# Moving the weight tiles of a three-stage kernel by 128 bytes in SBUF

## The chip, the cores and the metric

One Trainium2 chip, one core. The metric is the device time of one execution in microseconds; the kernel before takes 1165.19 us in the median of three runs (1164.79 to 1169.47). Lower is better.

## What is computed

Two sequences of 4096 positions with 192 channels go through a causal convolution with 7 taps per head (the taps are a softmax over the given weights), and then through two feed-forward layers, one with SiLU and one with ELU, each with an inner width of 2048. Everything is float32.

```python
w = softmax(weight, axis=-1)                      # 8 heads x 7 taps
out = einsum('hk,bskhg->bshg', w, windows(x, 7))  # causal, 24 channels a head
x = out.reshape(8192, 192)
h = x @ w_in;  x = (h * sigmoid(h)) @ w_out       # layer 0
h = x @ w_in2; x = elu(h) @ w_out2                # layer 1
```

## The kernel before

**Tiling.** The 8192 positions are cut into NB = 16 blocks of TB = 512 (`b`). The inner width 2048 is cut into NQ = 8 parts of 256 (`q`). A unit is one (layer, b, q); there are 2 x 16 x 8 = 256 units, and they run layer by layer, block by block, part by part. The loop near the end of the file issues, for each step, the input products of one unit and the output products of the unit two steps earlier (LAG = 2).

**Products.** Each number is held as a high and a low part in the type float32r, so that a product is built from three products of parts. `in_products` (L297, the matmul at L309) makes 9 matmuls for each half of the rows, `out_products` (L339, the matmul at L352) 10; a step of the loop therefore has 2 x 19 = 38 matmuls. Each multiplies 64 rows: one stream uses partitions 0 to 63, the other partitions 64 to 127, and matmuls of the two streams are issued in turn (`products`), so that one of each is under way. Each has a stationary operand (`lhsT`) of 64 partitions x 128 float32 columns, loaded by an instruction of its own, LDWEIGHTS (engine PEld in the rows), and a moving operand (`rhs`) of 64 partitions x 512 float32 columns. The whole program has 256 x 38 + 20 = 9748 matmuls, 20 of them in `warm` (L511).

**Operands.** The stationary operands are slices of the weight tiles `wi` and `wo`, the moving ones slices of `x_hl` (layer input) for L309 and of `g_hi` and `g_lo` (activations, high and low part) for L352. ScalarE and VectorE make `g_hi` and `g_lo` from the PSUM tile `h`.

**Weights on their way.** `load_w` (L83) brings float64 words into a `raw` tile by DMA. `decode_steps` (L97) turns them into float32: ScalarE writes the magnitude into `mag` (L109), VectorE builds the value in `val` (L112, L115, L119). `split_w` (L129) writes the high part to `wi` or `wo` with ScalarE (L126, L140) and the low part with GpSimd or VectorE (L127, L142). For parts 3 to 6 of layer 1 the value is built in other tiles, `val_g` (from the pool `tmp`) and `val_x` (from `xin`).

**Places in SBUF.** Tiles of a partition lie one behind the other in the order of the pools (L58 to L68), each rounded up to 32 bytes: `const` (with `tap_m`, `tap_s`, `tap_r` last), `wts`, `raw`, `mag_p`, `dec`, `xin`, `xs`, `out_p`, `mid`, `gp`, `tmp`. The pool `wts` starts at 416 modulo 512. A `wi` or `wo` tile has 2 x 384 x 4 = 3072 bytes, six times 512, so all 18 of them, and every 128-column slice of them (512 bytes), start at 416 modulo 512. So do the `raw` tiles (6144 bytes each), `mag` and the `val` tiles (3072 bytes each) and the first `x_raw` tile. The two `x_raw` tiles of 4160 bytes move the place on by 128, so `xs` and everything behind it start at 32 modulo 512: `x_hl`, `g_hi`, `g_lo`, `val_g`, whose slices of 512 columns have 2048 bytes, four times 512. Every moving operand thus starts at 32 modulo 512, every stationary operand at 416.

Of the kernel before, what the change touches and what calls it, by code (L numbers as in the profile page):

```python
# [9 lines left out]
F32 = mybir.dt.float32  # L10
# [12 lines left out]
P = 128  # L23
# [6 lines left out]
W_IN = 3 * P  # L30
W_OUT = 2 * D
RAW = 3

PLACES = NQ + 1


@with_exitstack
def kernel(
# [19 lines left out]
    const = ctx.enter_context(tc.tile_pool(name="const", bufs=1))  # L58
    wts = ctx.enter_context(tc.tile_pool(name="wts", bufs=1))
    raw = ctx.enter_context(tc.tile_pool(name="raw", bufs=RAW))  # L60
    mag_p = ctx.enter_context(tc.tile_pool(name="mag_p", bufs=1))
# [19 lines left out]
    IN, OUT, BOTH = slice(0, W_IN), slice(W_IN, W_IN + W_OUT), slice(0, W_IN + W_OUT)  # L81
# [11 lines left out]
    def words(layer, q, cols):  # L93
        w = raw_t[layer, q].bitcast(I32).rearrange("p (n two) -> p n two", two=2)
        return w[:, cols, 0], w[:, cols, 1]

    def decode_steps(layer, q, cols, val=None, mag=None):  # L97


        if (layer, q) not in dec_t:  # L100
            if mag is None:
                mag = mag_p.tile([P, W_IN + W_OUT], F32, tag="mag", name="mag")
            if val is None:
                val = dec.tile([P, W_IN + W_OUT], I32, tag="val", name="val")
            dec_t[layer, q] = mag, val
        mag, val = (t[:, cols] for t in dec_t[layer, q])
        lower, upper = words(layer, q, cols)
        return [
            lambda: nc.scalar.activation(  # L109
                out=mag, in_=upper.bitcast(F32), func=ACTF.Abs, scale=2.0**-112  # L110
            ),
            lambda: nc.vector.tensor_scalar(  # L112
                out=val, in0=lower, scalar1=29, scalar2=None, op0=ALU.logical_shift_right
            ),
            lambda: nc.vector.scalar_tensor_tensor(  # L115
                out=val, in0=upper, scalar=-(2**31), in1=val,
                op0=ALU.bitwise_and, op1=ALU.bitwise_or,
            ),
            lambda: nc.vector.scalar_tensor_tensor(  # L119
                out=val, in0=mag.bitcast(I32), scalar=3, in1=val,  # L120
                op0=ALU.logical_shift_left, op1=ALU.bitwise_or,
            ),
        ]
# [5 lines left out]
    def split_w(layer, q, cols, eng):  # L129
        if (layer, q) not in wt:  # L130
            wt[layer, q] = [
                wts.tile([P, 2, n], F32R, tag=f"{t}{(layer * NQ + q) % PLACES}", name=t)
                for t, n in (("wi", W_IN), ("wo", W_OUT))
# [13 lines left out]
    tap_raw = const.tile([P, 2, TAPS], F32, name="tap_raw")  # L147
    tap_e = const.tile([P, 2, TAPS], F32, name="tap_e")
    tap_w = const.tile([P, 2, TAPS], F32, name="tap_w")
    tap_m = const.tile([P, 2], F32, name="tap_m")  # L150
    tap_s = const.tile([P, 2], F32, name="tap_s")
    tap_r = const.tile([P, 2], F32, name="tap_r")

# [264 lines left out]
    def next_w(layer, q, *others, val=None):  # L418
        run(decode_steps(layer, q, BOTH, val), *others)
        if q + RAW < NQ:  # L420
            load_w(layer, q + RAW)
# [7 lines left out]
    def first_step(q):  # L429
        steps_w[q] = decode_steps(0, q, BOTH)  # L430
        return steps_w[q][1]
# [36 lines left out]
    base = where[0, NB - 1, 0]  # L468
    spare = PLACES - NQ
    for q in range(NQ):  # L470
# [11 lines left out]
    with tc.manual_schedule():  # L482
# [7 lines left out]
        ab = conv_steps(0, 0, lambda: ps_h.tile([P, 2, TB], F32, tag="h", name="conv")[:, 0, :])  # L490
        c, c_1 = conv_pool_steps(0, 1), conv_pool_steps(1, 1)
        d_in, d_out = (decode_steps(0, 0, cols) for cols in (IN, OUT))
        run(ab, c)
        run(c_1[:4])
# [122 lines left out]
```

## Time and profile before

| | before |
|---|---|
| median of 3 runs | 1165.19 us (1164.79 to 1169.47) |
| profiled execution, span from first to last instruction | 1167.4 us |
| matmuls under way (PE) | 1143.8 us, 98% |
| weight loads under way (PEld) | 942.9 us, 81% |
| VectorE, ScalarE, GpSimd busy | 70%, 55%, 5% |
| mean granted clock of TensorE | 0.998 |
| share of the chain that ended last | TensorE 96% |

All rows below are of one profiled execution. PE is TensorE's matmuls and PEld its weight loads, which overlap them; L309 is line 309 of the kernel; `h<-x_hl,wi` names what is written and what is read; 64*128 are the active rows and columns and 64x512 the shape that is read. Two matmuls are always under way, one of each stream, so what counts is how far apart the starts of one stream are, not how long a matmul's own row is.

### The profile page before, as it was taken

The page shows a single profiled execution, that of the slowest core. Times are in us where ns is not written, and L with a number is a line of the kernel's source. Part 1 is how long each engine was busy: PE and PEld are TensorE (multiplying, and loading weights), DVE is VectorE, ACT ScalarE, POOL GpSimd, SP SyncE. Part 2 cuts the span into 40 slices and gives each one's busy share as a digit, 9 for nine tenths or more (in the row PEclk, how much of TensorE's full clock was granted, in tenths as well). Part 3 has the DMA queues.
Part 4 walks back from the last instruction along what each step waited for, and adds up shares of the span by engine and source line. Part 5 has one row for each costly group of instructions (what it writes and reads, how often), then busy time and mean ns, then how long its engine had stood idle before and what let it go on. Part 6 is the DMA issues. An engine that isn't in the chain of part 4 may idle for free.

```text
span 1167.4 us, 22505 instructions
## 1 busy us (share of the span) xinstructions
PE 1143.8 (98%) x9748; PEld 942.9 (81%) x9748; DVE 819.8 (70%) x957; ACT 645.2 (55%) x761; POOL 57.5 (5%) x67
## 2 busy tenths in 40 slices
PE   4899999999999999999999999999999999999998
PEld 3799999977777777777789777777777777777776
DVE  8965546556556555567767787877878777787876
ACT  7655455555545555456775455555455554555554
POOL 7500000000000000000320000000000000000000
PEclk9999999999999999999999999999999999999999
DMA  6310111110111110152300111101111101111100
GB/s 189 105 47 9 34 42 42 42 37 6 42 42 42 42 25 18 42 136 82 83 10 29 33 42 42 42 16 35 33 42 42 42 15 28 42 42 42 30 22 19
DMA packets 31188, 51.11 MB, mean 44 GB/s; under 512 B 3952, under 2 KB 13936, under 8 KB 31088
## 3 DMA queue, kind: packets, MB, share of 16 engines
q1 hardware_dynamic: 31088, 49.67, 16.5%
q8 instruction: 76, 1.25, 0.5%
q14 instruction: 24, 0.20, 0.1%
HBM read 18.98 MB, written 6.29 MB: 22 GB/s over the span
## 4 chain that ended last, share of the span: by engine, by line
PE 96%; DVE 2%; issue 0%; SPq 0%; DMA 0%; ACT 0%; POOL 0%; DVEq 0%
PE h L309 46%; PE ab L352 30%; PE c L352 20%; DVE val L112 0%; DVE val L115 0%; DVE g_lo L337 0%; DMA raw<-in_w_dram 0%; DVE x_hl L127 0%; SPq L187 0%; DVE val L119 0%; DVE conv L268 0%; SPq L87 0%; POOL wi L127 0%; ACT x_hl L126 0%; DVE x_hl L229 0%
## 5 line engine op out<-in xcount | busy, mean ns | idle before, releaser
L309 PE MATMUL h<-x_hl,wi 64*128 64x512 f32 x4608 | 747.1, 394 | 19.7 <-ACT wi L126 13.5
L309 PEld LDWEIGHTS h<-x_hl,wi 64*128 64x128 f32 x4608 | 566.5, 184 | 116.5 <-ACT wi L126 13.9
L352 PE MATMUL ab<-g_hi,wo 64*128 64x512 f32 x2048 | 445.2, 392 | 0.0
L352 PEld LDWEIGHTS ab<-g_hi,wo 64*128 64x128 f32 x2048 | 319.7, 184 | 41.3
L352 PE MATMUL c<-g_lo,wo 64*128 64x512 f32 x1024 | 305.7, 392 | 0.0
L352 PE MATMUL c<-g_hi,wo 64*128 64x512 f32 x1024 | 305.4, 392 | 0.0
L352 PE MATMUL ab<-g_lo,wo 64*128 64x512 f32 x1024 | 305.4, 392 | 0.0
L337 DVE TENSOR_TENSOR g_lo<-h,g_hi 128x1024 fp32r<-128x1024 f32 x128 | 156.6, 1223 | 175.4 <-ACT h L326 175.3
L325 ACT ACTIVATE g_hi<-h 128x1024 fp32r<-128x1024 f32 x128 | 131.3, 1026 | 241.5 <-PE h L309 241.5
L330 ACT ACTIVATE g<-h 128x1024 f32<-128x1024 f32 x128 | 131.7, 1029 | 238.8 <-PE h L309 237.0
L332 DVE SCALAR_TENSOR_TENSOR g<-g,h 128x1024 f32<-128x1024 f32 x128 | 156.0, 1219 | 91.2 <-ACT g L331 90.9
L352 PEld LDWEIGHTS c<-g_hi,wo 64*128 64x128 f32 x1024 | 182.4, 184 | 20.7
L352 PEld LDWEIGHTS c<-g_lo,wo 64*128 64x128 f32 x1024 | 182.4, 184 | 20.6
L352 PEld LDWEIGHTS ab<-g_lo,wo 64*128 64x128 f32 x1024 | 182.4, 184 | 20.5
L337 DVE TENSOR_TENSOR g_lo<-g,g_hi 128x1024 fp32r<-128x1024 f32 x128 | 156.9, 1226 | 4.5
L331 ACT ACTIVATE g<-g 128x1024 f32<-128x1024 f32 x128 | 135.9, 1061 | 3.5
L326 ACT ACTIVATE h<-h 128x1024 f32<-128x1024 f32 x128 | 130.8, 1022 | 0.0
L268 DVE SCALAR_TENSOR_TENSOR conv<-x_raw,tap_w,conv 128x512 f32<-128x512 f32 (+1 forms) x180 | 106.0, 628 | 0.5
L335 DVE CAST g_hi<-g 128x1024 fp32r<-128x1024 f32 x128 | 88.8, 694 | 4.5
L374 DVE TENSOR_TENSOR both<-c,both 128x512 f32<-128x512 f32 x32 | 22.1, 692 | 52.2 <-ACT both L373 52.2
L127 POOL TENSOR_TENSOR wi<-val,wi 128x384 fp32r<-128x384 f32 x11 | 11.6, 1055 | 532.0 <-ACT wi L126 532.0
L127 DVE TENSOR_TENSOR x_hl<-conv,x_hl 64x256 fp32r<-64x256 f32 (+1 forms) x47 | 23.9, 534 | 1.2 <-ACT x_hl L126 0.7
(61 smaller groups left out, 325.3 us busy)
## 6 DMA issues: line engine op xcount, KB each, us to landing
x_hl<-x_hl SPq DMA_DIRECT2D x76, 256.0 KB, 3.9
raw<-in_w_dram SPq DMA_DIRECT2D x16, 512.0 KB, 4.4
x_hl<-x_hl SPq DMA_DIRECT2D x34, 128.0 KB, 3.7
x_raw<-in_xT_dram SPq DMA_DIRECT2D x16, 259.0 KB, 3.8
raw<-in_w_dram SPq DMA_DIRECT2D x32, 128.0 KB, 3.2
out_dram<-o SPq DMA_DIRECT2D x16, 256.0 KB, 2.0
x_raw<-in_xT_dram SPq DMA_DIRECT2D x32, 65.5 KB, 3.0
out_dram<-other SPq DMA_DIRECT2D x16, 128.0 KB, 2.3
```

The lines of the kernel that those rows point to most:

```text
L127: eng.tensor_sub(out=lo, in0=src, in1=hi.bitcast(F32))
L268: nc.vector.scalar_tensor_tensor(out=y, in0=x, scalar=w, in1=y, op0=ALU.mult, op1=ALU.add)
L309: nc.tensor.matmul(out=h[:, r, :], lhsT=w[ROWS[r], w_lo, ts(of, P)], rhs=x[ROWS[r], 3 * x_lo + part, :], start=n == 0, stop=n == len(order ...
L325: lambda: nc.scalar.activation(out=hi, in_=h, func=ACTF.Silu),
L326: lambda: nc.scalar.activation(out=g, in_=h, func=ACTF.Silu),
L330: lambda: nc.scalar.activation(out=g, in_=h, func=ACTF.Relu, scale=-1.0),
L331: lambda: nc.scalar.activation(out=g, in_=g, func=ACTF.Exp, scale=-1.0),
L332: lambda: nc.vector.scalar_tensor_tensor(out=g, in0=g, scalar=-1.0, in1=h, op0=ALU.add, op1=ALU.max),
L335: lambda: nc.vector.tensor_copy(out=hi, in_=g),
L337: return steps + [lambda: nc.vector.tensor_sub(out=lo, in0=g, in1=hi.bitcast(F32))]
L352: nc.tensor.matmul(out=acc_t[layer, b, f"{name}{r}"], lhsT=wo[ROWS[r], i, cols], rhs=hi_lo[part][ROWS[r], i, :], start=q == 0 and n in (0, ...
L374: nc.vector.tensor_add(out=to[:, cols], in0=halves[1][:, cols], in1=to[:, cols])
```

## The change

The tile `tap_m` in the pool `const` grows by 128 bytes per partition; only its first two elements are used, as before. Everything behind it moves on by 128 bytes: `tap_s`, `tap_r`, the weight tiles, the `raw` tiles and the start of `mag`. The tile `mag` grows by 3 x 128 = 384 bytes, which are not used. The tiles behind `mag` thus move by 128 + 384 = 512 bytes and keep their place modulo 512. No instruction is added, removed or moved, and no shape changes.

```diff
@@ -32,6 +32,7 @@
 RAW = 3
 
 PLACES = NQ + 1
+LINE = 128
 
@@ -99,7 +100,8 @@
         if (layer, q) not in dec_t:
             if mag is None:
-                mag = mag_p.tile([P, W_IN + W_OUT], F32, tag="mag", name="mag")
+                mag = mag_p.tile([P, W_IN + W_OUT + 3 * LINE // 4], F32, tag="mag", name="mag")
+                mag = mag[:, BOTH]
@@ -147,7 +149,7 @@
-    tap_m = const.tile([P, 2], F32, name="tap_m")
+    tap_m = const.tile([P, 2 + LINE // 4], F32, name="tap_m")[:, 0:2]
```

## Rows read from the trace of the kernel before

**Rows 1.** The page's span, and busy time of each engine.
```profile
span 1167.4 us, 22505 instructions
PE 1143.8 (98%) x9748; PEld 942.9 (81%) x9748; DVE 819.8 (70%) x957; ACT 645.2 (55%) x761; POOL 57.5 (5%) x67
```
**Rows 2.** The page's chain that ended last, share by engine, then by line.
```profile
PE 96%; DVE 2%; issue 0%; SPq 0%; DMA 0%; ACT 0%; POOL 0%; DVEq 0%
...
PE h L309 46%; PE ab L352 30%; PE c L352 20%; DVE val L112 0%; DVE val L115 0%; DVE g_lo L337 0%; DMA raw<-in_w_dram 0%; DVE x_hl L127 0%; SPq L187 0%; DVE val L119 0%; DVE conv L268 0%; SPq L87 0%; POOL wi L127 0%; ACT x_hl L126 0%; DVE x_hl L229 0%
```
**Rows 3.** The chain in order of time: start us, length us, engine, line.
```profile
5.52 4.26 DMA raw<-in_w_dram
...
54.87 2.12 PE h L309 x12
...
63.76 2.10 PE h L309 x18
68.19 2.10 PE h L309 x18
...
613.49 1.63 PE h L309 x14
617.92 1.64 PE h L309 x14
```
**Rows 4.** Stretches: length, busy us (instructions) by engine, granted clock, DMA share, GB/s.
```profile
0.00:30.00 30.00, 14.31 (x82) 10.68 (x84) 25.75 (x35) 22.19 (x40) 21.94 (x28) 0.94 0.65 184
300.00:600.00 300.00, 300.00 (x2574) 238.17 (x2572) 180.10 (x238) 168.76 (x206) 18.58 (x21) 1.00 0.19 50
600.00:900.00 300.00, 300.00 (x2574) 244.90 (x2572) 241.31 (x250) 166.46 (x182) 2.15 (x3) 1.00 0.14 35
```
**Rows 5.** Timeline of the last matmuls: start us, length us, engine, line, count.
```profile
1162.60 0.86 PE L352 MATMUL ab<-g_lo,wo 64*128 64x512 f32 x4
```
**Rows 6.** A stretch at half clock (columns as in rows 4), and its matmul timeline.
```profile
23.00:24.90 1.90, 1.90 (x11) 1.56 (x10) 1.80 (x3) 1.66 (x3) 1.90 (x2) 0.50 0.72 254
...
23.64 0.65 PE L309 MATMUL h<-x_hl,wi 64*128 64x512 f32 x2
...
24.07 0.65 PE L309 MATMUL h<-x_hl,wi 64*128 64x512 f32 x2
```
**Rows 7.** Timeline after a pause: weight loads and matmuls of both streams together.
```profile
21.68 0.19 PEld L309 LDWEIGHTS h<-x_hl,wi 64*128 64x128 f32 x2 [2.82 <-POOL wi L127]
...
21.79 0.19 PEld L309 LDWEIGHTS h<-x_hl,wi 64*128 64x128 f32 x2
...
22.02 0.57 PE L309 MATMUL h<-x_hl,wi 64*128 64x512 f32 x2
```
**Rows 8.** Timeline of matmuls in the steady part.
```profile
299.94 0.39 PE L352 MATMUL c<-g_hi,wo 64*128 64x512 f32 x1
299.96 0.40 PE L309 MATMUL h<-x_hl,wi 64*128 64x512 f32 x1
300.17 0.39 PE L352 MATMUL c<-g_hi,wo 64*128 64x512 f32 x1
300.20 0.39 PE L309 MATMUL h<-x_hl,wi 64*128 64x512 f32 x1
```
**Rows 9.** Timeline of weight loads at the same moment.
```profile
299.97 0.18 PEld L309 LDWEIGHTS h<-x_hl,wi 64*128 64x128 f32 x1
299.97 0.18 PEld L352 LDWEIGHTS c<-g_hi,wo 64*128 64x128 f32 x1
```
**Rows 10.** Instructions on `val`, then on `val_g`, 470 to 640 us: ns min/median/max.
```profile
L115 DVE SCALAR_TENSOR_TENSOR val<-raw,val x4: 959/960/1378, 514.7 to 584.1; 128x768 int32<-128x768 int32 x4
L127 POOL TENSOR_TENSOR wi<-val,wi x4: 1019/1022/1025, 520.6 to 601.2; 128x384 fp32r<-128x384 f32 x4
...
L115 DVE SCALAR_TENSOR_TENSOR val_g<-raw,val_g x2: 958/958/959, 552.8 to 557.3; 128x768 int32<-128x768 int32 x2
L127 POOL TENSOR_TENSOR wi<-val_g,wi x2: 1022/1024/1026, 578.2 to 582.7; 128x384 fp32r<-128x384 f32 x2
```

## The prediction, made before the change was run

> **What bounds the kernel now.** I read the page first: matmuls are under way for 1143.8 of 1167.4 us [rows 1]. A busy PE alone says little, so the chain that ended last comes next: 96% of it is TensorE, split over the two matmul lines and over nothing else of weight [rows 2]. The chain in order of time shows where TensorE starts to be alone on it: from 54.87 us [rows 3] to the end of the last matmuls at 1162.60 + 0.86 = 1163.46 us [rows 5], 1108.6 us. Ahead of that lies the start-up, behind it 1167.4 - 1163.5 = 3.9 us of tail. So the time is 54.9 us, plus a number of matmuls by their pace, plus 3.9 us.
>
> The pace: one step of the loop has 19 matmuls in each of the two streams. In the chain, steps start at 63.76 and 68.19 us, and much later at 613.49 and 617.92 us [rows 3], 4.43 us both times, so one matmul per stream each 4.43 / 19 = 0.2332 us. The stretches agree: 2574 matmuls touch a window of 300 us, some three of which began before it, so 300 / (2571 / 2) = 0.2334 us [rows 4]. I take 0.2333 us: 1108.6 / 0.2333 = 4752 turns of both streams. **One nanosecond per turn is 4.75 us, 0.41% of the time.** That is the lever of this change, which touches an operand of every matmul.
>
> What makes up the 233.3 ns? At half the clock (granted 0.50, the 1.2 GHz level) one stream's matmuls start at 23.64 and 24.07 us [rows 6], 0.43 us apart: 512 columns at 1.2 GHz are 426.7 ns, so there is nothing besides the streaming of the moving operand. At 2.4 GHz the same 512 columns would be 213.3 ns. So 233.3 - 213.3 = **20.0 ns of each turn are something other than streaming**, 20.0 x 4752 = 95 us in all. That is the most that any change of the operands' reading can give back.
>
> **The change part by part.** Instructions, shapes, queues, waits and their order stay the same, so no wait appears and nothing is moved past another. Three kinds of tile start elsewhere modulo 512.
>
> *Weight tiles, written.* ScalarE, GpSimd and VectorE write `wi` and `wo`, the last ones of the start-up ahead of TensorE. How these engines take to a place can be read: `val` lies at 416 and `val_g` at 32 modulo 512, the very two places of this change. The decode step L115 takes at least 959 ns on the one and 958 ns on the other, GpSimd's L127 reads the one in a median of 1022 ns and the other in 1024 ns [rows 10]. (The 1378 ns maximum is an execution beside GpSimd's work, so the minimum is the row to compare.) The difference is 0.2% at most; on the 54.9 us of start-up that is 0.1 us. I take nothing.
>
> *`raw` and `mag`, `tap_s` and `tap_r`.* The same engines read and write them, with the same answer. The DMA into `raw` is the one access for which no row has another place; the first load that the chain waits for takes 4.26 us [rows 3]. If it changed by a tenth either way, an estimate as wide as I can defend, this would be 0.4 us. I take nothing, and 0.4 us for either end. Later loads run while TensorE is the bound.
>
> *Weight tiles, read by TensorE.* This is the term that decides, and no row shows weights at another place, so it has to be bounded. Below: all of the 20.0 ns go, -95 us. Above: in each turn the load's first 128 bytes hold up the stream while it walks 128 bytes, 32 of its columns, 32 / 512 x 213.3 = 13.3 ns, +63 us. Which value in between?
>
> First, is the load what a matmul waits for? After a pause the loads start at 21.68 us, and at 21.79 us, 0.11 us later, the next loads are already let in [rows 7], which in the steady part happens as a matmul begins. So a load needs about 0.11 us to let its matmul begin, while the following matmuls start at 22.02 us, 0.23 us after their loads [rows 7]. In the steady part the loads of both streams start at 299.97 us and are recorded for 0.18 us, and their matmuls start at 300.17 and 300.20 us [rows 8, 9], 0.02 and 0.05 us after the record ends. A load that took a few nanoseconds more or less would be covered by this; what covers it is the matmul of the same stream that is still streaming. If the 0.02 us is not slack but a fixed way from load to matmul, that cover is gone and each nanosecond of the load costs its 4.75 us.
>
> Second, does it matter where the load stands against the stream? The change moves the weights by 128 bytes against the moving operand. The stream covers 128 bytes in 13.3 ns, so a load that starts 13.3 ns later against its stream would meet it about as a shifted one does. Such a case is in the trace: the stream of L352 starts its matmul at 299.94 us and its next load 0.03 us later; the stream of L309 starts at 299.96 us and its load 0.01 us later [rows 8, 9]. The two stand 0.02 us apart in this, more than the change's 13.3 ns, and both take 0.23 to 0.24 us to their next matmul. They are issued in turn, so they can't run far apart, and this is no proof; but neither holds the other up by nanoseconds that could be seen over a step.
>
> Third, does another access to SBUF change the pace? VectorE is busy for 180 us of one window and for 241 us of the next, on tiles at the same places as the moving operands, and both windows hold the same 2574 matmuls [rows 4].
>
> Each says that the pace doesn't hang on which bytes are read beside it. The nearest row is the equal pace under two offsets, so I take 0 ns per turn and keep both ends.
>
> The sum: 54.9 + 4752 x 0.2333 + 3.9 = 1167.4 us for the profiled execution, with 0 us of change. That execution is 2.2 us, 0.2%, over the median of the three runs, inside their spread; for a run I say the median, 1165.2 us.
>
> **The rivals.** *Faster: the 20 ns are a meeting of load and stream.* Stream and load of one row of the array read the same partitions at once, the stream from 32 and the load from 416 modulo 512. If places that differ by a multiple of 128 bytes share something, starting both at 32 could let them keep out of each other's way. For it: 20 ns that don't show at half the clock, where everything has time to spare, look like something being fed too slowly. Against it: the three readings above. Price: a quarter of the 20 ns, since the change moves the offset by one quarter of 512 bytes, is 5 ns, -24 us, 1141 us; all of it is 1070 us. Chance 0.30: 0.19 between 1141 and 1159.4 us, 0.11 below 1141.
>
> The Trainium skill, page "TensorE: Matmul & The Clock Gate", section "Back-to-back issue gap", gives a gap of N / 2.4 + 2.5 ns, 216 ns for 512 columns. By that rule 17.5 ns of the 233.3 here should not be there, and with them gone the time would be about 1165.2 - 17.5 x 4752 / 1000 = 1082 us, an estimate from that page. The trace doesn't show that pace at the full clock anywhere.
>
> *Slower: the loads run into the stream.* With both at 32, the first columns of a load and of a moving operand lie in the same 128 bytes of the 512, and the loads begin 0.01 to 0.03 us after their streams [rows 8, 9]. It decides once the stream itself is held, not only the load; a load held by less than 0.02 us costs nothing by the cover above. Price: the same 5 ns as its mirror, +24 us, 1189 us; at the bound of 13.3 ns it is 1228 us. For it: an equal start is the one case in which the two begin in the same place every time. Against it: the stream walks through 512 bytes in 53 ns, so whatever the start it passes all places of a load. Chance 0.22: 0.13 between 1171 and 1189 us, 0.09 above.
>
> *The change does nothing to the weights,* because what counts is a place of finer grain: 416 and 32 are both 32 modulo 128. This ends where the forecast ends, at 1165 us, and is part of it.
>
> **How the numbers follow.** No change: 0.48. Faster 0.30, slower 0.22. About 0.5% is what a measurement of this kernel can tell from no change: 1159.4 to 1171.0 us. The likeliest case gives the time, 1165.2 us; its own range is that band, which holds the 0.4 us of start-up and the 0.4% spread of the runs. The range reaches to the quarter prices, 1141 to 1189 us, and leaves out 0.11 below and 0.09 above; the bounds of 1070 and 1228 us lie in what is left out.
>
> **What would show it.** Right: the steps of the chain stay 4.43 us apart and a 300 us window still holds 2574 matmuls. The faster rival shows as a step under 4.41 us, the slower as one over 4.45 us, from the first steps on and in both layers alike, with the loads' 0.18 us or their distance to the next matmul changed by as much. If the steps stay and the time moves, it is the start-up: TensorE's lone stretch would begin elsewhere than at 54.87 us. What would make the prediction wrong above all is that the 0.02 us between load and matmul is no slack.

## The result, and the profile after

The change makes the kernel faster by 2.4%: 1137.95 us in the median (1137.65 to 1138.84) against 1165.22 us (1164.79 to 1169.47), a ratio of 0.9763 with a 95% interval of 0.9747 to 0.9780. The forecast was no change, 1165.2 us, with a range down to 1141 us.

The page of the changed kernel, span and busy time, answers to [rows 1]:

```profile
span 1136.4 us, 22505 instructions
PE 1111.5 (98%) x9748; PEld 917.1 (81%) x9748; DVE 818.4 (72%) x957; ACT 643.0 (57%) x761; POOL 56.8 (5%) x67
```

The same instructions, 31.0 us less. VectorE and ScalarE are about as busy as before (1.4 and 2.2 us less); TensorE's two rows have shrunk by 32 and 26 us. The chain in order of time (start us, length us, engine, line) answers to [rows 3]:

```profile
55.26 2.09 PE h L311 x16
59.62 2.04 PE h L311 x18
63.93 2.04 PE h L311 x18
...
296.49 2.04 PE h L311 x18
300.79 2.04 PE h L311 x18
...
1129.52 2.81 PE ab L354 x24
```

TensorE is alone on the chain from 55.26 us, 0.4 us later than before, so the start-up has gained nothing. The steps are 4.31 us apart, where they were 4.43 us. The stretches (length, busy us and instructions by engine, granted clock, DMA share, GB/s) answer to [rows 4]:

```profile
0.00:30.00 30.00, 13.63 (x80) 9.93 (x82) 25.02 (x35) 22.09 (x40) 21.24 (x28) 0.94 0.61 184
300.00:600.00 300.00, 300.00 (x2650) 247.96 (x2648) 190.28 (x247) 175.63 (x216) 20.71 (x24) 1.00 0.21 53
600.00:900.00 300.00, 300.00 (x2650) 247.92 (x2650) 244.71 (x253) 169.11 (x185) 0.00 (x0) 1.00 0.13 34
```

A window of 300 us now holds 2650 matmuls instead of 2574, at the same granted clock of 1.00. The mean distance between starts of one stream in the trace is 226.67 ns, in both layers, against 233.33 ns: 6.66 ns less per turn. (A turn is one matmul of each stream; 4752 turns is the prediction's count.) 4752 turns x 6.66 ns = 31.6 us; less 0.4 us of a later start and 0.2 us of a longer tail that is the 31.0 us between the two profiled executions.

Why do the medians differ by 27.3 us and not by 31? The kernel before has two paces. A span is about 1.8 us shorter than the time of its run (1136.4 us and 1138.22 us in the changed kernel), so the profiled execution before, with its span of 1167.4 us, took about 1169.2 us and was not one near the median. An early stretch of it shows the other pace:

```profile
60.00:200.00 140.00, 140.00 (x1207) 134.60 (x1205) 79.20 (x112) 72.86 (x88) 0.00 (x0) 1.00 0.15 35
```

1203 matmuls start in these 140 us, 232.8 ns per turn in the mean. Followed one by one, one stream starts its matmuls 232.4 ns apart and the other 233.3 ns. So the first runs ahead, until at 227 us it is 0.72 us in front, three turns and a little; from there on both go at 233.3 ns. At 300 us one stream begins its output products with the first of these lines, the other with the second:

```profile
299.94 0.39 PE L352 MATMUL c<-g_hi,wo 64*128 64x512 f32 x1
...
300.67 0.39 PE L352 MATMUL c<-g_hi,wo 64*128 64x512 f32 x1
```

Executions of the kernel before end near 1165.0 or near 1169.5 us, with nothing between; 4752 turns at 232.4 ns against 226.7 give 27 us and at 233.3 ns 31 us. The trace of the kernel before is of the slower kind. For the faster kind there is the trace of the kernel with weights at 160 below, at the same distance between weights and moving operands, from a run of 1165.26 us: both its streams go at 232.4 ns throughout. In the changed kernel's trace there is one pace, and its four times lie within 1.2 us.

### The profile page after: what moved, and what is told of

The parts are those of the page before. It is cut to its first block, busy times and chain, and to the rows that moved or that the text cites. A ratio compares the mean times of both kernels' runs of the same rounds, so it can differ in the third digit from the quotient of the medians.

```text
span 1136.4 us, 22505 instructions
## 1 busy us (share of the span) xinstructions
PE 1111.5 (98%) x9748; PEld 917.1 (81%) x9748; DVE 818.4 (72%) x957; ACT 643.0 (57%) x761; POOL 56.8 (5%) x67
## 4 chain that ended last, share of the span: by engine, by line
PE 95%; DVE 2%; SPq 1%; DMA 1%; issue 0%; POOL 0%; ACT 0%; DVEq 0%
PE h L311 45%; PE ab L354 30%; PE c L354 20%; DVE g_lo L339 1%; DVE val L117 0%; DMA raw<-in_w_dram 0%; DVE val L114 0%; DVE val L121 0%; SPq L189 0%; DMA x_raw<-in_xT_dram 0%; SPq L88 0%; POOL wo L144 0%; DVE conv L270 0%; DVE x_hl L129 0%; POOL wi L129 0%
## 5 line engine op out<-in xcount | busy, mean ns | idle before, releaser
L311 PE MATMUL h<-x_hl,wi 64*128 64x512 f32 x4608 | 569.0, 388 | 20.8 <-ACT wi L128 14.8
L311 PEld LDWEIGHTS h<-x_hl,wi 64*128 64x128 f32 x4608 | 434.4, 185 | 114.7 <-ACT wi L128 15.7
L354 PE MATMUL ab<-g_hi,wo 64*128 64x512 f32 x2048 | 273.9, 386 | 0.0
L354 PEld LDWEIGHTS ab<-g_hi,wo 64*128 64x128 f32 x2048 | 192.3, 184 | 39.9
L354 PE MATMUL c<-g_lo,wo 64*128 64x512 f32 x1024 | 157.9, 386 | 0.0
L354 PE MATMUL c<-g_hi,wo 64*128 64x512 f32 x1024 | 157.9, 386 | 0.0
L354 PE MATMUL ab<-g_lo,wo 64*128 64x512 f32 x1024 | 157.8, 386 | 0.0
L354 PEld LDWEIGHTS ab<-g_lo,wo 64*128 64x128 f32 x1024 | 96.2, 184 | 19.9
L354 PEld LDWEIGHTS c<-g_hi,wo 64*128 64x128 f32 x1024 | 96.2, 184 | 19.9
L354 PEld LDWEIGHTS c<-g_lo,wo 64*128 64x128 f32 x1024 | 96.1, 184 | 20.0 <-DVE g_lo L339 0.2
```

Of the source, the lines that this page charges most:

```text
L311: nc.tensor.matmul(out=h[:, r, :], lhsT=w[ROWS[r], w_lo, ts(of, P)], rhs=x[ROWS[r], 3 * x_lo + part, :], start=n == 0, stop=n == len(order ...
L354: nc.tensor.matmul(out=acc_t[layer, b, f"{name}{r}"], lhsT=wo[ROWS[r], i, cols], rhs=hi_lo[part][ROWS[r], i, :], start=q == 0 and n in (0, ...
```

## The experiments

Each expectation stands as it was written before its run. "Distance" is the place of the stationary operands less that of the moving ones, modulo 256 bytes. The pace is the mean time between starts of one stream, from the trace. Cuts in the code are marked `...`.

### Which place counts: four layouts

The first three change the two sizes of the change, here for the first; the others in the same way:

```diff
-    tap_m = const.tile([P, 2], F32, name="tap_m")
+    tap_m = const.tile([P, 2 + 256 // 4], F32, name="tap_m")[:, 0:2]
 ...
-                mag = mag_p.tile([P, W_IN + W_OUT], F32, tag="mag", name="mag")
+                mag = mag_p.tile([P, W_IN + W_OUT + 256 // 4], F32, tag="mag", name="mag")
+                mag = mag[:, BOTH]
```

**Weights at 160.** 

> Weight tiles at 160 modulo 512, moving operands stay at 32. Theory R (what counts is the weights' place relative to the moving operand, best when equal): the pace is not the 226.7 ns per turn of the changed kernel but nearer 233 ns, 1160 us or more. Theory W (what counts is the weights' own place, 416 is a bad one): no reason against 226.7 ns, about 1138 us.

**Weights at 288** (384 and 128 bytes). 

> Weight tiles at 288 modulo 512, moving operands stay at 32, so half of 512 bytes apart. Theory R: slower than the changed kernel, pace near 233 ns, 1160 us or more; if R is a matter of distance, 288 is at least as slow as 416. Theory W: no reason against 226.7 ns, about 1138 us.

**Both at 416** (0 and 384 bytes). 

> Weight tiles stay at 416 as before the change, and the moving operands are moved there too, to 416 modulo 512. Theory R: equal places, so 226.7 ns per turn and 1138 us. Theory W: weights at 416 as before, so 233.3 ns and 1165 us.

**Only `raw` and `mag` moved** (128 unused bytes in the last `wo` tile, 384 in `mag`).

```diff
-                wts.tile([P, 2, n], F32R, tag=f"{t}{(layer * NQ + q) % PLACES}", name=t)
-                for t, n in (("wi", W_IN), ("wo", W_OUT))
+                wts.tile([P, 2 * n + 32 * (k == 2 * PLACES - 1)], F32R, ...)[:, 0 : 2 * n].rearrange(...)
+                for t, n, k in (("wi", W_IN, ...), ("wo", W_OUT, ...))
```

> Only the raw tiles and mag move to 32 modulo 512, weights stay at 416 and moving operands at 32. Theories R and W: nothing of TensorE's reading is changed, 233.3 ns per turn and 1165 us. A rival in which the decode's and the DMA's places count: part of the 27 us is gained here, below 1160 us.

Measured: at 160 no change (1165.3 to 1169.9 us, ratio 1.0019, 0.9998 to 1.0039); at 288 1138.05 us (0.9744, 0.9694 to 0.9795); both at 416 1138.15 us (0.9745, 0.9695 to 0.9795); `raw` and `mag` alone no change (ratio 1.0004, 0.9980 to 1.0028). The stretch from 300 to 600 us of the third:

```profile
300.00:600.00 300.00, 300.00 (x2650) 248.04 (x2648) 190.25 (x247) 175.68 (x216) 20.71 (x24) 1.00 0.21 53
```

and of the fourth:

```profile
300.00:600.00 300.00, 300.00 (x2574) 240.99 (x2572) 179.98 (x238) 168.85 (x206) 18.56 (x21) 1.00 0.20 50
```

Weights at 416 are no bad place: with the moving operands at 416 too, the window holds the changed kernel's 2650 matmuls. Theory W falls with this run and with the one at 160. Theory R stands, but not as it was written: it expected 288 to be slow, and 288 against 32 is as fast as equal places, so what counts goes by the distance modulo 256. The decode and the DMA's target have no part in it.

### The distance in between

Same edit with 192 and 320 bytes, 160 and 352, 320 and 192, and 96 and 384.

> Weights at 96, moving operands at 32 modulo 512: 64 bytes apart. So far the distance modulo 256 decides: 0 gave 226.7 ns per turn, 128 gave 232.4 to 233.3. Theory S (load and stream meet more or less, the cost grows with the distance up to 128): about 229 to 231 ns, 1148 to 1157 us. Theory H (two halves of 128 bytes, in or out): 226.7 ns and 1138 us or 233 ns and 1165 us, nothing between.

> Weights at 64, moving operands at 32: 32 bytes apart. Theory S: about 228 ns, 1143 us. Theory H: 226.7 or 233 ns as for 64 bytes apart, the same one if the border lies between 64 and 128.

> Weights at 224, moving operands at 32: 192 bytes apart, which is 64 behind modulo 256. If only the amount of the distance counts, the same as with weights at 96; if the sign counts (the load ahead of or behind the stream), another time: the later it meets the stream, the worse, up to 233 ns, 1165 us.

> Weights and moving operands both at 0 modulo 512, so that no slice lies across a border of 512, 256, 128 or 64 bytes. Theory D (the distance alone counts): 226.7 ns per turn, 1138 us, as with both at 32 and both at 416. Rival A (crossing a border costs part of the remaining 13.3 ns over streaming): below 226 ns, under 1135 us.

| weights / moving operands modulo 512 | distance | matmuls in 300 to 600 us | pace, ns | median, us |
|---|---|---|---|---|
| 32 / 32 (changed kernel) | 0 | 2650 | 226.7 | 1137.95 |
| 288 / 32 | 0 | 2650 | 226.7 | 1138.05 |
| 416 / 416 | 0 | 2650 | 226.7 | 1138.15 |
| 0 / 0 | 0 | 2650 | 226.7 | 1137.77 |
| 64 / 32 | 32 | 2576 | 233.3 | 1169.38 |
| 96 / 32 | 64 | 2574 | 233.3 | 1169.46 |
| 160 / 32 | 128 | 2586 | 232.4 (run of 1165.26 us) | 1165.3 or 1169.6 |
| 416 / 32 (kernel before) | 128 | 2574 | 232.4 and 233.3, then 233.3 | 1165.22 |
| 224 / 32 | 192 | 2624 | 228.9 | 1148.56 |

Theory S (a cost growing with the distance) falls with the first row at 32 bytes: it costs as much as 64. Theory H (nothing between) falls with 192 bytes, 0.9832 of the time before (0.9772 to 0.9893). Modulo 256 that is 64 bytes to the other side, and it is faster than 64, so the side counts too. Both at 0, where no slice crosses a border, gains nothing over both at 32, so rival A falls too. One line of that run says more; its stretch from 300 to 600 us:

```profile
300.00:600.00 300.00, 300.00 (x2650) 283.49 (x2648) 190.55 (x247) 175.61 (x217) 20.72 (x24) 1.00 0.20 53
```

Weight loads are under way for 283 us instead of 248: here the two streams run 30 ns apart, so that their loads of 184 ns together cover 214 ns of a turn, while in the changed kernel they run 3 ns apart and cover 187 ns. The pace is the same. That points to something inside one stream, which a run below tests.

### Every distance in steps of 8 bytes, in one kernel

In the changed kernel the slice that is loaded begins further on, block by block.

```diff
+    def shifted(start, n):
+        return slice(start + n - 64 * (start == 2 * P and n > 0), start + n - 64 * (start == 2 * P and n > 0) + P)
 ...
-                out=h[:, r, :], lhsT=w[ROWS[r], w_lo, ts(of, P)],
+                out=h[:, r, :], lhsT=w[ROWS[r], w_lo, shifted(of * P, 2 * (16 * layer + b))],
 ...
-                out=acc_t[layer, b, f"{name}{r}"], lhsT=wo[ROWS[r], i, cols],
+                out=acc_t[layer, b, f"{name}{r}"], lhsT=wo[ROWS[r], i, shifted(cols.start, 2 * (16 * layer + b))],
```

> The changed kernel, but in each of the 32 blocks of the two layers the stationary slice begins further on, by 8 bytes per block: distance from the moving operand 0 bytes in block 0 of layer 0, 8 in block 1, up to 248 in block 15 of layer 1 (the last slice of a tile goes back by 256 bytes more). So it multiplies by wrong columns; the work is the same. Known points of whole kernels: 0: 226.7 ns per turn, 32 and 64: 233.3, 128: 232.4 to 233.3, 192: 228.9. Theory S (a cost that grows with the distance up to 128 and falls behind it) is already unlikely; theory J (a jump just behind 0 and a slow return) expects 233 ns from the first 8 to 32 bytes on up to about 130 to 160 bytes, then a fall over 228.9 ns at 192 to 226.7 ns at 248. If some distance lies below 226.7 ns, there is a better version; if each is at least 226.7 ns, the other 13.3 ns over streaming don't depend on the place. Steps of a block are 4.31 us at 226.7 ns and 4.43 us at 233.3 ns.

Then 120 bytes in the whole kernel (`shifted(..., 30)`), and the sweep from 248 bytes down to 0 (`62 - 2 * (16 * layer + b)`):

> The changed kernel with every stationary slice 120 bytes further on than the moving operand's place (it multiplies by wrong columns; the work is the same). In the sweep the block at 120 bytes went at 226.7 ns per turn between neighbours at 233.4 and 232.5. Theory P (the pace belongs to the distance): 226.7 ns in the whole kernel, about 1138 us. Rival Q (the pace is a state that the run of matmuls falls into and keeps, and 120 was lucky): 230 to 233 ns, 1150 us or more.

> The sweep over the distances the other way round: 248 bytes in the first block down to 0 in the last (wrong columns again). Theory P: each distance has the pace that it had going up: 226.7 ns at 0 and 120, 233.3 at 32, 40, 64, 72, 228.4 to 229 at 240 and 192. Rival Q: another pace in many blocks, since each is entered from another side.

Each of these runs is one execution. Pace of each block in ns, going up / going down; one number where they agree within 0.2 ns (0 going up and 248 going down lie in the start-up):

| bytes | +0 | +8 | +16 | +24 | +32 | +40 | +48 | +56 |
|---|---|---|---|---|---|---|---|---|
| 0 | - / 226.7 | 230.7 | 233.3 | 230.0 / 231.2 | 233.4 | **233.3 / 226.8** | 233.3 | 233.3 |
| 64 | 233.3 | 233.3 | 232.0 | 233.4 | 234.3 | 233.3 | 233.3 | **226.7** |
| 128 | 232.5 / 233.3 | 233.4 | 233.4 | 231.2 | 233.3 | 233.3 | 230.1 | 232.0 |
| 192 | 228.9 | 230.7 | 231.9 | 232.2 | 233.3 | 231.1 | 228.4 | 233.3 (up) |

The kernel at 120 bytes throughout took 1138.21 us at 226.7 ns. Of the 30 distances from 8 to 240 bytes, met from both sides, 27 keep their pace within 0.2 ns, so theory P holds for them; theory J's smooth return does not: neighbours 8 bytes apart can differ by 6.6 ns. Three distances have two paces. The clearest is 40 bytes. Its steps in the chain, going up:

```profile
218.91 2.10 PE h L315 x18
223.35 2.10 PE h L315 x18
227.78 2.10 PE h L315 x18
```

and going down:

```profile
959.13 2.04 PE h L315 x18
963.44 2.04 PE h L315 x18
967.75 2.04 PE h L315 x18
```

4.43 against 4.31 us for the same distance: there the distance alone does not settle the pace, as rival Q says. Whether it depends on what went before is not shown: the way back also puts every distance into the other layer. At 128 bytes the layer is not the reason, since whole kernels keep 232.4 ns (weights at 160) or 233.3 ns (`raw` and `mag` moved) through both. None of the distances goes below 226.67 ns, so none of them is a better place than the change's.

### Which load, and whose stream

```diff
-                out=h[:, r, :], lhsT=w[ROWS[r], w_lo, ts(of, P)],
+                out=h[:, r, :], lhsT=w[ROWS[r], w_lo, shifted(of * P, 32 * (b % 4 // (1 + r) % 2))],
```

and the same for `wo`: one stream's loads, the other's, or both moved by 128 bytes.

> The changed kernel, but the slices of one stream or both begin 128 bytes further on (so it multiplies by wrong columns): blocks 0, 4, 8, 12 neither, 1, 5, 9, 13 the stream of partitions 0 to 63, 2, 6, 10, 14 the stream of partitions 64 to 127, 3, 7, 11, 15 both. Theory O (a load gets in the way of the stream in its own partitions): a shift in one stream alone slows that stream, and as they are issued in turn both go at its pace, 232.4 to 233.3 ns per turn in three blocks of four and 226.7 ns in the fourth. Rival X (load of one stream against the moving operand of the other): the same for both alone. Rival Z (what counts is that both loads or both streams differ): one alone differs from both.

The chain's steps from a block with only the stream of partitions 0 to 63 moved into one with only the other moved:

```profile
370.35 1.63 PE h L315 x14
374.77 1.86 PE h L315 x14
...
392.23 2.04 PE h L315 x17
396.53 2.04 PE h L315 x18
...
405.20 2.09 PE h L315 x18
409.62 2.09 PE h L315 x18
```

The chain goes by whichever stream comes last, so its steps (4.42 us, in the middle of the second block 4.30 us, then 4.42 us again) have to be taken apart by streams. From the third step of a block on (the first two still hold output products of the block before), the stream whose slices are moved takes 4.42 us per step (4.43 us in some early blocks) and the other 4.31 us, its step with none moved. They shift against each other by 110 ns per step. When the faster one is about 0.48 us in front, it goes at 4.42 us as well, as in the last steps of the first block. In the step from 667.7 us, with only the stream of partitions 64 to 127 moved, one stream starts its matmuls 226, 227, 227 ns apart all along, the other 241, 233, 231, 231, 229, 230, 232 and so on. So each stream has a pace of its own, and rival Z falls. Which is which? In each step the first load with `wi` that carries a wait belongs to the stream that is issued first, that of partitions 0 to 63; in the changed kernel, where the loads of a pair start 3 ns apart, it is the first of its pair in all 256 units. In such blocks it stands in the fast stream (at 672.0 us: 227, 227, 226 ns follow), in blocks with that stream moved in the slow one (at 636.9 us: 231, 231, 229, 230, 232, 241 ns). So it is the stream's own loads, as theory O says, and rival X falls with Z. O's number, one pace for both, holds only where the lead is used up.

Then `wi` in odd blocks, `wo` in blocks 2 and 3 modulo 4, both streams (`32 * (b % 2)` and `32 * (b % 4 // 2)`):

> The changed kernel, but the slices of wi or wo or both begin 128 bytes further on (so it multiplies by wrong columns): wi in odd blocks, wo in blocks with remainder 2 or 3 modulo 4. Theory L (each load costs by its own distance, turn by turn): a step of 9 turns with wi and 10 with wo takes 19 x 226.7 = 4.31 us with none, 9 x 233.3 + 10 x 226.7 = 4.37 us with wi alone, 4.37 us with wo alone, 4.42 to 4.43 us with both. Rival G (the pace is a state of the whole run of matmuls, set by any slow load): wi alone and wo alone already take 4.42 to 4.43 us.

Steps with none, `wi` alone, `wo` alone and both:

```profile
323.13 2.04 PE h L315 x18
327.43 2.04 PE h L315 x18
...
358.07 2.11 PE h L315 x18
362.49 2.11 PE h L315 x18
...
393.15 2.06 PE h L315 x18
397.55 2.06 PE h L315 x18
...
428.39 2.09 PE h L315 x18
432.79 2.10 PE h L315 x18
```

4.30, 4.42, 4.40 and 4.40 us here; in the mean over the blocks 4.31, 4.43, 4.39 and 4.42 us. L expected 4.37 us for either alone, G 4.42 to 4.43 us: G is right for `wi`, and `wo` lies between. The turns of one stream with `wo` alone, in ns, mean over the inner steps of such blocks, show why:

```
matmuls with wi: 228 233 231 227 227 227 227 227 233 | with wo: 241 233 231 232 228 230 233 241 233 236
```

The pace falls to 227 ns some turns after the `wo` loads have ended, and it is lost again at the last matmul with `wi`, the one during which the first `wo` slice is loaded. So it is **the load under way, the next matmul's**, with which the cost begins, as L says. But with `wi` alone the ten matmuls on good `wo` slices never settle (235, 233, 236, 224, 231 ns and so on): the disturbance outlasts its cause, and the prices don't add up load by load.

### Narrower loads

```diff
+    def width(b, less):
+        return (128, 96, 64, 32)[b % 4] if less else P
 ...
-                out=h[:, r, :], lhsT=w[ROWS[r], w_lo, ts(of, P)],
+                out=h[0 : width(b, 0 < n < 8), r, :],
+                lhsT=w[ROWS[r], w_lo, columns(of * P, layer, b, 0 < n < 8)],
```

and likewise for `wo`; `columns` adds 32 columns in layer 1.

> The changed kernel with narrower loads in most matmuls: 128, 96, 64 and 32 stationary columns in blocks 0, 1, 2, 3 modulo 4 (it leaves out the other columns of the products, so the result is not the reference's); in layer 1 the slices begin 128 bytes further on. Theory C (the cost is a meeting of load and stream, so it goes with what is loaded): in layer 1 the pace falls from 233 ns with 128 columns toward layer 0's, and in layer 0 from 226.7 ns, the fewer columns the more, down to 213 to 216 ns if all of the 20 ns were the load's. Rival F (13.3 ns are a fixed price of a matmul): layer 0 stays at 226.7 ns whatever the width, and layer 1 comes down to 226.7 ns at most.

The load groups by shape (busy us, mean ns of one):

```profile
L320 PEld LDWEIGHTS h<-x_hl,wi 64*128 64x128 f32 x1920 | 183.1, 187 | 80.5 <-ACT wi L128 14.1 <-POOL wi L129 2.5 <-ACT g_hi L337 2.2
L320 PEld LDWEIGHTS h<-x_hl,wi 64*96 64x96 f32 x896 | 72.2, 158 | 29.3
L320 PEld LDWEIGHTS h<-x_hl,wi 64*64 64x64 f32 x896 | 60.3, 131 | 39.3
L320 PEld LDWEIGHTS h<-x_hl,wi 64*32 64x32 f32 x896 | 48.3, 105 | 49.9
```

Loads get shorter by 26 to 29 ns for each 32 columns (the 187 ns hold some loads at half the clock; in the steady part it is 184 ns), and the pace doesn't follow: 226.7, 230.3, 229.6 and 230.3 ns for 128, 96, 64 and 32 columns in layer 0, 233.1, 230.9, 230.2 and 231.0 ns in layer 1 (230.9 is the mean of one block at 228.6 ns and three at 231.7). At the good distance narrower loads are slower, at the bad one somewhat faster. Theory C (the cost goes with what is loaded) falls in layer 0, and rival F (226.7 ns whatever the width) with it.

## Why the prediction was wrong

**Right:** the frame. TensorE is the bound, one nanosecond per turn is 4.75 us (measured 31.6 us for 6.66 ns), the start-up and the moved `raw` and `mag` cost next to nothing (0.4 us later, and no change when moved alone), and the term left open, how TensorE reads its weights, was the one that decided.

**Wrong: the value of that term,** 0 ns instead of -6.66 ns. It fails in the second of the three readings, "does it matter where the load stands against the stream". I took a load that starts 0.02 us later against its stream for a stand-in for a load 128 bytes further on, and the equal pace of the two streams [rows 8, 9] for a sign that neither matters. The equal pace was the pace of the slower one: in the same trace the streams go at 232.4 and 233.3 ns until one is 0.72 us in front, and equally only from then on. So "they can't run far apart" is wrong by three turns, and the caveat that I hung on it was not weighed. And shifting in time is not shifting in place: with `raw` and `mag` alone moved, both streams' loads start 0.003 us after their streams, where one of them started 0.03 us after it in the steady part of the kernel before [rows 8, 9], and the pace is 233.3 ns in both; 32 bytes of place cost 6.6 ns. The three times held a hint that I read as spread: two near 1165 us and one at 1169.47 us are the two paces. And the 2.2 us "over the median" set a span against a run's time; the profiled execution took about 1169.2 us, 4 us over the median.

The first reading fails as a bound as well. That a load's record ends 0.02 to 0.05 us ahead of its matmul was taken as cover; narrower loads end up to 0.08 us earlier and win nothing at the good distance, and the change left the loads at 184 ns. So the end of the load is not what the matmul waits for, and a cost can arise without it. The third reading is true and beside the point: the pace is the same whether VectorE is busy for 190 or 245 of 300 us, but TensorE's own two readings are another matter.

On this point the Trainium skill, page "TensorE: Matmul & The Clock Gate", section "Step-by-step: what each phase is for", says that loading the next weights takes no SBUF bandwidth from the running matmul, since TensorE has two read ports of its own. Read as "a load doesn't disturb the running matmul", it doesn't hold here: with the next load's slice in another place the same matmuls go 6.66 ns per turn slower. The measurement decides; whether what is lost is SBUF bandwidth no run shows.

**The rivals.** The faster one came: the pace hangs on the place of the load against its stream. It was given 0.30, of which 0.11 for less than 1141 us, where the 1138 us lie. That load and stream meet at something that they share is its reason and was not shown. Its price was mis-sized: a quarter of the 20.0 ns, 5 ns, was taken for a quarter of 512 bytes; measured was a third, 6.66 ns, and the sweep shows that the cost is not in proportion to the offset. Its grain of 128 bytes is wrong as well: 32 bytes cost as much as 64. The slower rival's mechanism, an equal start as the worst case, is wrong in sign. "A finer grain, 32 modulo 128" as a reason for no effect is refuted by the result itself, and by the row at 32 bytes.

**What stays open.** The cause inside the chip. Shown is that a stream's pace depends on the place of its own next weights against its own moving operand, modulo 256 bytes in the layouts tried, that it takes values from 226.7 to 234.3 ns irregularly, and that three distances have two paces. Why 6.66 ns, why a layout takes one of its two paces, why 40 and 120 bytes can be as good as 0, and whether the 13.3 ns left over pure streaming have to do with loads, these runs don't tell; the narrower loads speak against a simple count of bytes read twice at once.

## What to carry to other kernels

Where matmuls with a load each bound the time, compare the distance between starts of one stream with the same at half the clock: what is over half of that is not streaming. Then try the stationary tiles at the same place as the moving operands modulo 256 bytes; it costs padding alone, and was worth 2.4% here. Take no offset in time, and no quiet neighbour engine, as evidence on an offset in place: measure the place itself, several in one kernel if need be.

## What the runs showed of the hardware that was not expected

- The pace of a stream of 64-row float32r matmuls with 512 columns and a load each depends on the place of the loaded slice relative to the moving one: 226.7 ns at distance 0, 233.3 ns at 32 and 64 bytes, 228.9 ns at 192.
- The time between starts is a pattern of several turns, not a constant: at 128 bytes it runs 228, 230, 233, 241, 232, 231, 232 ns and repeats, or 229 and 238 in turn. At 24, 40 and 128 bytes two patterns were met.
- The two streams have separate paces and can shift against each other, by 110 ns within one step of the loop, although they are issued in turn. The faster one came to be 0.72 us in front in the kernel before, 0.48 us where one stream was moved, and went at the other's pace from there on.
- At half the clock the 20 ns are not there [rows 6]; at the full clock none of the places tried brought a turn below 226.67 ns.
